# Landing buffers of v apart, three chunks' transposed keys in another PSUM bank, p's sum in PSUM, and a new order of all jobs

## The chip, the core and the metric

The kernel runs on one core of a Trainium2 chip. The core has TensorE (matmuls and their weight loads), VectorE, ScalarE, GpSimd and SyncE, whose queue issues most of the DMAs. The metric is the device time of one execution in microseconds, the median of several runs.

## The reference

Two stages. An attention with a decaying state, and a mixture of four experts over its output:

```python
# r, k, v: (4, 8, 768, 48) f32; w, u: (8, 48)
for t in range(S):
    kt, vt, rt = k[:, :, t], v[:, :, t], r[:, :, t]
    cur = einsum('bhd,bhe->bhde', u[None] * kt, vt)
    y[:, :, t] = einsum('bhd,bhde->bhe', rt, state + cur)
    state = w[None, :, :, None] * state + einsum('bhd,bhe->bhde', kt, vt)
x = y.transpose(0, 2, 1, 3).reshape(3072, 384)
p = domain_probs / (domain_probs.sum(-1, keepdims=True) + 1e-09)     # (3072, 4)
for e in range(4):                                                   # w1: (4, 384, 1024), w2: (4, 1024, 384)
    out += p[:, e:e + 1] * (maximum(x @ w1[e], 0.0) @ w2[e])
```

## The kernel before

The sequence is cut into 24 chunks ci of 128 tokens: batch ci % 4, position ci // 4, so chunks 0 to 3 are the first chunks of the four batches. Each chunk passes these jobs. Its r, k and v are loaded (Rt, Kt, Vt; 192 KB each). `scale` multiplies r and k by powers of w into RK_sb. `T` transposes them (keys are half 1, r half 0) on TensorE, by DMA from chunk 8 on, and `Tout` copies the result from PSUM to RKT in SBUF. `At` is the product of r and keys in the two banks of At_all, `mask` masks it into AtM (two halves, VectorE). `Y` multiplies it by v (Vb, a bf16 copy) and adds the state's part. The u term goes beside this: `ruk_a` (r times k), `ruk_b` (times u), both on GpSimd but for chunk 0, `dcoef` (a sum over 48, VectorE), `dv` (times v, GpSimd), and `Yout` adds dv to y. `Sm`, `Sv`, `S` advance the state.

The experts come in super-chunks of four chunks. For the first two, `X` transposes y on TensorE and `Xout` copies it to xTe. For later ones ScalarE multiplies y by p (`Xs`, line 621) and a DMA transposes each half of the result (`Xout`, line 632). `l1` is x @ w1 (hT_ps), `relu` runs on ScalarE, `l2` is h @ w2 (out_ps), `ev` multiplies it by p. The weights arrive in f32 in pieces of 3, 3 and 2 blocks (w1e0.1 is piece 1 of expert 0's w1) through four staging slots, and `cast` turns each piece into bf16. From the third super-chunk on, sums and differences of blocks replace some of the products. p is transposed (`pt`) and normalized (`pn`, lines 386 to 389) once.

PSUM has eight banks: two in At_all, one for transposes (tr), one for y, states and w (ys), and four general ones (mm). The general ones serve u, the powers of w, p, l1, l2, the transposed y and the filler matmuls alike. A buffer is handed on when the last reader of what was in it is done, which the waiting engine sees as a semaphore.

No engine chooses its next instruction. All 1437 jobs stand in one written list, PLAN; each entry is a job's number in base 62 and the letter of an engine (T TensorE, V VectorE, A ScalarE, P GpSimd, S SyncE's queue). Each engine works off its own entries in the list's order. SPINS puts filler matmuls ahead of named jobs on TensorE: n // 4 of 128x512 and n % 4 of 128x128. They compute nothing that is used. Planner tokens (slots, takes, drops) describe buffers to the program that made the list; the tiles' own buffer counts are in the pool calls. For the two kinds of landing buffers these are:

```python
                t = work.tile([128, H, D], F32, tag=n, bufs=NIN, name=n)
                    tl["in", ci] = work.tile([128, 2, H, D], F32, tag="in", bufs=NIN, name="RKin")
        load_job((n, ci), (0.965, 64), run, (("inp", ci),))
```

Of the kernel before, what the change touches and what calls it, by code (L numbers as in the profile page):

```python
# [18 lines left out]
def kernel(  # L19
# [28 lines left out]
    NIN = 4  # L48
    NRK = 4
# [82 lines left out]
    p_sum = consts.tile([128, TOTC, 1], F32)  # L132
# [70 lines left out]
    slots = dict(inp=NIN, wst=NST, RKT=4, AtM=2, Ysb=3, ruk=3, dv=3, Vb=4, At=2, tr=1, ys=1,  # L203
# [53 lines left out]
    def load_in(n, ci):  # L257
# [3 lines left out]
        def run():  # L261
            if n == "Vt":
                t = work.tile([128, H, D], F32, tag=n, bufs=NIN, name=n)
            else:
                if ("in", ci) not in tl:
                    tl["in", ci] = work.tile([128, 2, H, D], F32, tag="in", bufs=NIN, name="RKin")
                t = tl["in", ci][:, 1 if n == "Kt" else 0]
            tl[n, ci] = t
            nc.sync.dma_start(t, SRC[n][b, :, sl, :].transpose([1, 0, 2]))
        load_job((n, ci), (0.965, 64), run, (("inp", ci),))  # L270
# [108 lines left out]
    def c_pt():  # L379
        tl["pp"] = psum.tile([128, E, TOTC], F32, tag="mm", bufs=4, name="p_ps")  # L380
# [3 lines left out]
    def c_pn():  # L384
        pp = tl["pp"]
        nc.vector.reduce_sum(p_sum, pp.rearrange("p e n -> p n e"), axis=AX.X)
        nc.vector.tensor_scalar(p_sum, p_sum, scalar1=1e-9, scalar2=None, op0=ALU.add)
        nc.vector.reciprocal(p_rec, p_sum)
# [25 lines left out]
    def attention(ci):  # L414
# [43 lines left out]
        def vb(eng):  # L458
# [3 lines left out]
            rk - 0.3 if ci >= SUB else rk, (("Vb", ci),), (("inp", ci),))  # L462
# [10 lines left out]
        job(("dv", ci), {"P": 0.82}, dv, [("dcoef", ci), ("Vt", ci)], rk - 0.4, (("dv", ci),), (("inp", ci),))  # L473
# [9 lines left out]
        else:  # L483
            two = ci < SUB

            def tr(i):
                def run():
                    if two and i:
# [12 lines left out]
            for i in range(2):  # L501
                job(("T", ci, i), {"T": 0.23}, tr(i), [("scale", ci, i)], on_pe,
                    ((("At" if i and two else "tr"), "T", ci),) if i == 0 or two else (),
# [4 lines left out]
            def tout(i):  # L508
                def run(eng):
                    if ("RKT", ci) not in tl:  # L510
                        tl["RKT", ci] = work.tile([128, 2, NP, C], BF16, tag="RKT", bufs=4, name="RKT")
                    if parts == 2:
                        copy_on(eng, tl["RKT", ci][:, i], tl["T", ci, i])
                        if i:
# [4 lines left out]
            if parts == 2:  # L519
# [3 lines left out]
                    rk - 20, (("RKT", ci),), (("At", "T", ci),))  # L523
# [746 lines left out]
    for sc in ORDER_SC:  # L1270
# [11 lines left out]
        for q, m, x in SEQ_OF.get(sc, SEQ_P):  # L1282
# [100 lines left out]
```

## Time and profile before

| | us |
|---|---|
| median of 3 runs | 283.35 |
| lowest and highest run | 282.93, 283.63 |
| span of the profiled execution | 281.5 |
| median less span | 1.85 |
| TensorE busy in the span | 274.8 |
| VectorE, ScalarE, GpSimd busy | 201.3, 182.8, 109.9 |

The span goes from the first to the last instruction of the profiled execution; the device time of a run also holds what lies around it. Busy times are sums over instructions and filler matmuls count as busy.

### The profile page before, as it was taken

To read this page: it belongs to the slowest core of one execution; us is meant where nothing else is said; L and a number is where in the kernel's file an instruction comes from. 1 tells how busy PE (TensorE), PEld (TensorE's weight loads), DVE (VectorE), ACT (ScalarE), POOL (GpSimd) and SP (SyncE) were. 2 spreads that over 40 slices of the span, in tenths; PEclk is the share of its full clock that TensorE was granted. 3 is DMA by queue.
4 is the path that set the end of the run, shared out by engine and by line. 5 is a ranking of instruction groups with operands and counts; after the bars stand their busy time and mean duration, and the time that the engine had idled before them with its cause. 6 is when DMAs were issued, how large, how long until landed. Compare 5 with 4: busy or idle time off the path is not lost.

```text
span 281.5 us, 7035 instructions
## 1 busy us (share of the span) xinstructions
PE 274.8 (98%) x2817; PEld 196.7 (70%) x2817; DVE 201.3 (72%) x368; ACT 182.8 (65%) x350; POOL 109.9 (39%) x137
## 2 busy tenths in 40 slices
PE   7799999999999999999999999999999999999995
PEld 3478567767666454899445899554799644899995
DVE  4968877788798867577354888679996703795672
ACT  5586675888763689644789744688863688653320
POOL 4986334576365479315961425645210000000000
PEclk9999999999999999999999999999999999999999
DMA  7999998998999998678995389967364402000004
GB/s 149 241 307 333 266 325 242 235 245 199 256 197 168 204 207 189 96 145 153 176 179 151 86 157 157 151 138 159 86 88 86 140 2 56 0 2 2 2 15 156
DMA packets 133493, 43.25 MB, mean 154 GB/s; under 512 B 121658, under 2 KB 133436, under 8 KB 133460
## 3 DMA queue, kind: packets, MB, share of 16 engines
q1 hardware_dynamic: 133300, 42.74, 69.5%
q8 instruction: 22, 0.36, 0.6%
q14 instruction: 11, 0.09, 0.1%
q10 hardware_dynamic: 160, 0.05, 0.1%
HBM read 26.79 MB, written 4.72 MB: 112 GB/s over the span
## 4 chain that ended last, share of the span: by engine, by line
PE 93%; DVE 3%; DMA 1%; SPq 1%; ACT 1%; POOL 0%; issue 0%; DVEq 0%; ACTq 0%; POOLq 0%
PE hT_ps L761 35%; PE M_ps L986 26%; PE out_ps L791 7%; PE hT_ps L1216 4%; PE hT_ps L1250 4%; PE out_ps L1233 4%; PE M_two L1164 3%; PE At_all L545 2%; PE Y_ps L592 2%; DMA RKin<-in_r_dram 1%; PE hT_ps L755 1%; PE Y_ps L585 1%; PE St_ps L661 1%; PE At_all L1164 1%; DVE AtM L559 1%; PE At_ps L545 1%
## 5 line engine op out<-in xcount | busy, mean ns | idle before, releaser
L772 ACT ACTIVATE hAll<-hT_ps 128x512 bf16<-128x512 f32 x152 | 85.0, 598 | 19.1 <-PE hT_ps L761 17.1
L761 PE MATMUL hT_ps<-stg,w_sb 128*128 128x512 bf16 x384 | 86.7, 379 | 0.0
L761 PEld LDWEIGHTS <-w_sb 128*128 128x128 bf16 x456 | 42.2, 98 | 45.6
L986 PEld LDWEIGHTS <-hAll 128*128 128x128 bf16 x640 | 52.6, 98 | 1.0
L621 ACT ACTIVATE stg<-dv,p_nat 128x384 bf16<-128x384 f32 x72 | 41.3, 610 | 11.2 <-DMA stg<-stg 8.3
L445 POOL TENSOR_TENSOR ruk<-RKin 128x384 f32<-128x384 f32 x24 | 26.2, 1092 | 22.7 <-DMA RKin<-in_k_dram 16.2
L680 POOL TENSOR_TENSOR S<-Tn,wC 64x192 bf16<-64x192 f32 x32 | 22.4, 700 | 29.9 <-DVE Tn L670 22.0
L1023 ACT COPY o_sb<-M_ps 128x192 f32<-128x192 f32 x35 | 10.9, 316 | 33.7 <-PE M_ps L986 30.2
L986 PE MATMUL M_ps<-w_sb,hAll 128*128 128x192 bf16 x320 | 29.7, 246 | 0.0
L471 POOL TENSOR_TENSOR dv<-Vt,dcoef 128x384 f32<-128x384 f32 x24 | 22.0, 918 | 19.0 <-DVE dcoef L466 10.7
L453 POOL TENSOR_TENSOR ruk<-ruk,U_sd 128x384 f32<-128x384 f32 x23 | 24.1, 1055 | 0.9
L791 PE MATMUL out_ps<-w_sb,hAll 128*128 128x384 bf16 x128 | 22.9, 326 | 0.2 <-DVE p_nat L389 0.2
L934 DVE TENSOR_TENSOR hAll<-hAll 128x1024 bf16<-128x1024 bf16 (+1 forms) x28 | 22.0, 793 | 0.2
L433 DVE TENSOR_TENSOR RK_sb<-RKin,W_both 128x768 bf16<-128x768 f32 x16 | 18.0, 1125 | 1.3 <-DMA RKin<-in_r_dram 1.3
L83 POOL CAST Vb<-Vt 128x384 bf16<-128x384 f32 x16 | 9.1, 567 | 25.1 <-DMA Vt<-in_v_dram 17.2
L761 PE MATMUL hT_ps<-xTe,w_sb 128*128 128x512 bf16 x72 | 18.4, 380 | 0.0
L791 PEld LDWEIGHTS <-hAll 128*128 128x128 bf16 x128 | 12.2, 98 | 8.3 <-issue 0.4
L934 DVE TENSOR_TENSOR hAll<-stg,hAll 128x1024 bf16<-128x1024 bf16 (+1 forms) x14 | 10.5, 765 | 8.3 <-PE M_ps L986 8.0
L986 PE MATMUL M_ps<-w_mix,hAll 128*128 128x192 bf16 x160 | 16.5, 246 | 0.0
L562 DVE TENSOR_TENSOR AtM<-At_all,mask 128x1024 bf16<-128x1024 f32 x8 | 9.7, 1217 | 9.3 <-PE At_all L545 9.3
L986 PE MATMUL M_ps<-o_sb,hAll 128*128 128x192 bf16 x160 | 16.1, 246 | 0.0
L986 PE MATMUL M_ps<-w_sb,stg 128*128 128x192 bf16 x160 | 16.0, 246 | 0.0
(144 smaller groups left out, 440.3 us busy)
## 6 DMA issues: line engine op xcount, KB each, us to landing
stg<-in_moe_w_dram SPq DMA_DIRECT2D x16, 576.0 KB, 6.5
RKin<-in_k_dram SPq DMA_DIRECT2D x24, 192.0 KB, 4.2
Vt<-in_v_dram SPq DMA_DIRECT2D x24, 192.0 KB, 3.9
RKin<-in_r_dram SPq DMA_DIRECT2D x24, 192.0 KB, 3.9
out_dram<-o_sb SPq DMA_DIRECT2D x23, 192.0 KB, 2.3
stg<-in_moe_w_dram SPq DMA_DIRECT2D x8, 384.0 KB, 6.2
stg<-stg SPq DMA_TRANSPOSE x36, 3.1
RKT<-RK_sb SPq DMA_TRANSPOSE x16, 3.2
```

Source lines behind the costliest of these rows:

```text
L433: job(("scale", ci, 0), {"V": SCALE_US}, lambda: nc.vector.tensor_mul(RK[:, :, :, 0:D], tl["in", ci], W_both), [("Rt", ci), ("Kt", ci), (" ...
L445: nc.gpsimd.tensor_mul(tl["ruk", ci], tl["Rt", ci], tl["Kt", ci])
L453: nc.gpsimd.tensor_mul(tl["ruk", ci], tl["ruk", ci], U_sd)
L471: nc.gpsimd.tensor_mul(tl["dv", ci], tl["Vt", ci], tl["dcoef", ci].to_broadcast((128, H, D)))
L621: nc.scalar.mul(o, tl["Ysb", ci], p_nat[:, e, n_p:n_p + 1])
L680: nc.gpsimd.tensor_mul(S_new[pr, :, cl], Tn2[pr, tn_at[ci], :, cl], wC[pr, :, None].to_broadcast((P2, NP, D)))
L761: nc.tensor.matmul(ps[:, 0:n, :].rearrange("p a b -> p (a b)"), w1_sb[:, e, db, fb * 128:(fb + 1) * 128], xTe[:, x0 + db, s0:s0 + n, :].re ...
L772: nc.scalar.activation(hTs[:, fb, s0:s0 + n, :], ps[:, 0:n, :], AF.Relu)
L791: nc.tensor.matmul(ps, relu_tile(e, sc)[:, fb, s, :], w2_sb[:, e, fb, :], start=(fb == 0), stop=(fb == NFB - 1))
L934: nc.vector.tensor_tensor(o, x, y, op=op)
L986: nc.tensor.matmul(tl["P", sc, q, m], st, moving(m, hf, (n + 4) % 8), start=(opens and n == 0 and not (one_bank and m == 7)), stop=(hf == ...
L1164: nc.tensor.matmul(o, st[:, 2 * (3 - n // 2) + n % 2, :], mv, start=(x in ((1, 2) if own else (1,)) and n == 0), stop=(n == 7), skip_group ...
```

## The change

It has four parts. The planner's token inp is split into inp (r and k) and vin (v), with four buffers each. The transposed keys of chunks 1 to 3, which went to a free bank of At_all, go to a general bank. p's sum and the sum plus 1e-9 live in two more columns of p's PSUM tile instead of an SBUF tile. And PLAN and SPINS are new: the last 539 of the 1437 jobs stand in the same order as before, the others do not.

```diff
+    NV = 4
...
-    p_sum = consts.tile([128, TOTC, 1], F32)
...
-                t = work.tile([128, H, D], F32, tag=n, bufs=NIN, name=n)
+                t = work.tile([128, H, D], F32, tag=n, bufs=NV, name=n)
...
-        load_job((n, ci), (0.965, 64), run, (("inp", ci),))
+        load_job((n, ci), (0.965, 64), run, (("vin" if n == "Vt" else "inp", ci),))
...
-        tl["pp"] = psum.tile([128, E, TOTC], F32, tag="mm", bufs=4, name="p_ps")
+        tl["pp"] = psum.tile([128, E + 2, TOTC], F32, tag="mm", bufs=4, name="p_ps")
...
-        pp = tl["pp"]
-        nc.vector.reduce_sum(p_sum, pp.rearrange("p e n -> p n e"), axis=AX.X)
-        nc.vector.tensor_scalar(p_sum, p_sum, scalar1=1e-9, scalar2=None, op0=ALU.add)
-        nc.vector.reciprocal(p_rec, p_sum)
+        pp, p_sum = tl["pp"][:, 0:E], tl["pp"][:, E:E + 2]
+        nc.vector.reduce_sum(p_sum[:, 0].rearrange("p (n o) -> p n o", o=1), pp.rearrange("p e n -> p n e"), axis=AX.X)
+        nc.vector.tensor_scalar(p_sum[:, 1], p_sum[:, 0], scalar1=1e-9, scalar2=None, op0=ALU.add)
+        nc.vector.reciprocal(p_rec.rearrange("p n o -> p (n o)"), p_sum[:, 1])
...
+            own_bank = 0 < ci < SUB
...
-                    if two and i:
+                    if own_bank and i:
+                        tl["T", ci, 1] = psum.tile([128, NP, C], BF16, tag="mm", bufs=4, name="RKT_ps")
+                    elif two and i:
...
-                        if i:
+                        if i and not own_bank:
                             at_free.append(at_of[ci])
...
-    SPINS = {'wmm': 1, 'umm': 1, ('T', 0, 0): 10, ('At', 0): 8, ('T', 2, 0): 16, ('T', 1, 1): 2, ('Y', 0): 3,
-             ('At', 1): 2, ('T', 3, 1): 12, ('T', 2, 1): 4, ('Y', 1): 2, 'wt': 1, ('l1', 0, 0, 3, 0): 1, ('l1',
-             0, 0, 6, 1): 9, ('l1', 0, 0, 0, 0): 8}
+    SPINS = {'wmm': 1, 'umm': 1, ('T', 0, 1): 8, ('T', 0, 0): 8, ('At', 0): 14, ('T', 1, 0): 10, 'wt': 10,
+             ('T', 1, 1): 6, ('At', 1): 3, ('l1', 0, 0, 0, 3): 16}
```

The first three chunks' order changes from 0, 1, 2, 3 to 0, 3, 1, 2. The loads before were K0 V1 R1 R0 K1 R2 R3 V0 K3 K2 w1e0.1 w1e0.2 V2 w1e0.0 p V3 and so on; now they are K3 K0 R3 R0 V0 R1 V3 K1 w1e0.0 K2 p w1e0.1 R2 w1e0.2 V1 w2e0.0. Below are three places of the new order.

ScalarE's queue near the start of the program, before (after the two powers of w; U_sd is the copy of u, RKT the copies of transposed r and k, W_both those of the powers of w):

```order
L368 COPY U_sd_114<-u_ps_155 128x384
L79 COPY RKT_188<-RKT_ps_179 128x512
L366 COPY W_both_113<-W_ps_157 128x384
L366 COPY W_both_113<-W_ps_159 128x384
L79 COPY RKT_218<-RKT_ps_211 128x512
L79 CAST Vb_234<-Vt_161 128x384
L79 COPY RKT_249<-RKT_ps_229 128x512
L370 ACTIVATE hAll_72<-hAll_72 4x128
L79 COPY RKT_292<-RKT_ps_284 128x512
L79 COPY RKT_292<-At_all_120 128x512
L79 CAST w1_sb_70<-stg_73 128x3x384
```

The same place in the new order:

```order
L80 COPY RKT_183<-At_all_119 128x512
L366 COPY W_both_113<-W_ps_156 128x384
L366 COPY W_both_113<-W_ps_162 128x384
L80 COPY RKT_183<-RKT_ps_193 128x512
L80 COPY RKT_222<-RKT_ps_217 128x512
L80 CAST Vb_244<-Vt_139 128x384
L368 COPY U_sd_114<-u_ps_168 128x384
L370 ACTIVATE hAll_72<-hAll_72 4x128
L376 ACTIVATE wC_115<-wt_ps_269 128x4
L80 CAST Vb_272<-Vt_143 128x384
L80 CAST w1_sb_70<-stg_73 128x3x384
L80 COPY RKT_306<-RKT_ps_233 128x512
```

U_sd moved from the first place to the seventh, and chunk 0's keys (RKT_183 from At_all), which VectorE copied, stand ahead of the two copies of w; the first cast of w1 has fewer copies ahead.

VectorE's queue in the same stretch, before (AtM are the masks, y_sb the sums of y and dv, dcoef the u term's sums; p's four operations come some twenty instructions later):

```order
L466 TENSOR_REDUCE dcoef_192<-ruk_164 128x8
L428 TENSOR_TENSOR RK_sb_99<-RKin_146,W_ps_159 128x8x48
L559 TENSOR_TENSOR AtM_216<-At_all_120,mask_94 128x512
L428 TENSOR_TENSOR RK_sb_99<-RKin_150,W_ps_159 128x8x48
L559 TENSOR_TENSOR AtM_216<-At_all_120,mask_94 128x512
L81 COPY RKT_218<-At_all_120 128x512
L466 TENSOR_REDUCE dcoef_269<-ruk_185 128x8
L559 TENSOR_TENSOR AtM_290<-At_all_120,mask_94 128x512 x2
L607 TENSOR_TENSOR y_sb_121<-Y_ps_258,dv_239 128x384
L81 COPY RKT_249<-At_all_120 128x512
L607 TENSOR_TENSOR y_sb_121<-Y_ps_324,dv_304 128x384
```

The same place in the new order:

```order
L466 TENSOR_REDUCE dcoef_214<-ruk_137 128x8
L428 TENSOR_TENSOR RK_sb_99<-RKin_141,W_ps_162 128x8x48
L562 TENSOR_TENSOR AtM_224<-At_all_119,mask_94 128x512 x2
L82 COPY RKT_222<-RKT_ps_239 128x512
L610 TENSOR_TENSOR y_sb_120<-Y_ps_248,dv_257 128x384
L466 TENSOR_REDUCE dcoef_275<-ruk_178 128x8
L562 TENSOR_TENSOR AtM_285<-At_all_119,mask_94 128x512 x2
L82 COPY xTe_312<-xT_ps_308 128x3x128
L82 COPY RKT_306<-RKT_ps_293 128x512
L610 TENSOR_TENSOR y_sb_120<-Y_ps_321,dv_298 128x384
L386 TENSOR_REDUCE p_ps_315<-p_ps_315 128x24
L387 TENSOR_SCALAR p_ps_315<-p_ps_315 128x24
```

Chunk 0's two masks follow each other and its y comes right behind them, ahead of the next chunk's masks; p's operations follow the second chunk's y.

SyncE's queue in the first third of the program, before. L478 are DMA transposes of RK for chunks 11 and 10 and then 13 and 12, L632 those of y times p; the single L632 is the second half of chunk 9, the last one that the third super-chunk's l1 needs:

```order
L632 DMA_TRANSPOSE stg_73<-stg_73 128x6x128 x2
L269 DMA RKin_1591<-in_k_dram 128x8x48
L478 DMA_TRANSPOSE RKT_1603<-RK_sb_99 128x8x128
L269 DMA Vt_1621<-in_v_dram 128x8x48
L269 DMA RKin_1591<-in_r_dram 128x8x48
L632 DMA_TRANSPOSE stg_73<-stg_73 128x6x128
L269 DMA Vt_1646<-in_v_dram 128x8x48
```

The same place in the new order, where the single L635 is the second half of chunk 9 and the two L478 are chunks 10 and 11:

```order
L635 DMA_TRANSPOSE stg_73<-stg_73 128x6x128 x2
L269 DMA Vt_1601<-in_v_dram 128x8x48
L829 DMA out_0_dram<-o_sb_121 128x384
L269 DMA RKin_1624<-in_r_dram 128x8x48
L269 DMA RKin_1624<-in_k_dram 128x8x48
L635 DMA_TRANSPOSE stg_73<-stg_73 128x6x128
L829 DMA out_0_dram<-o_sb_121 128x384
L478 DMA_TRANSPOSE RKT_1674<-RK_sb_99 128x8x128
L478 DMA_TRANSPOSE RKT_1676<-RK_sb_99 128x8x128
```

The RKT transposes of chunks 10 and 11 moved behind chunk 9's second half, and a store of the output stands ahead of it. On TensorE, the first l1 group that reads that half (expert 2 of the third super-chunk) was the twelfth group of the super-chunk and is now the seventh.

## Rows read from the trace of the kernel before

**Rows 1.** Windows of the whole span; columns are named in the first line.

```profile
core 0: us, PE busy (x) PEld busy (x) DVE busy (x) ACT busy (x) POOL busy (x), PEclk, DMA share, GB/s
0.00:16.00 16.00, 12.43 (x104) 6.38 (x106) 10.60 (x29) 8.99 (x16) 11.49 (x23) 1.00 0.92 209
16.00:26.20 10.20, 10.03 (x160) 8.61 (x161) 8.07 (x19) 8.67 (x20) 6.99 (x8) 1.00 1.10 316
26.20:278.60 252.40, 252.35 (x2555) 181.68 (x2554) 182.37 (x321) 165.04 (x316) 91.41 (x108) 1.00 0.68 144
```

**Rows 2.** Windows, filler matmuls alone: us, busy (x), granted clock, DMA share, GB/s.

```profile
0.00:26.20 26.20, 9.59 (x38) 1.00 0.99 251
```

**Rows 3.** Timeline of TensorE: start, duration, instruction, idle before it and its releaser.

```profile
8.58 0.40 PE L545 MATMUL At_all<-RKT 64*128 64x128 bf16 x8 [0.36 <-DVE RKT L81]
...
13.93 0.38 PE L497 MATMUL At_all<-ident,RK_sb 128*128 128x128 bf16 x4 [0.41 <-DVE AtM L559]
...
14.99 0.38 PE L497 MATMUL At_all<-ident,RK_sb 128*128 128x128 bf16 x4 [0.46 <-ACT RKT L79]
...
16.84 0.67 PE L755 MATMUL hT_ps<-xTe,w_sb 128*128 128x128 bf16 x9
...
26.23 1.14 PE L791 MATMUL out_ps<-w_sb,hAll 128*128 128x384 bf16 x6 [0.19 <-DVE p_nat L389]
```

**Rows 4.** Timeline of VectorE, the first 26 us.

```profile
6.55 1.02 DVE L428 TENSOR_TENSOR RK_sb<-RKin,W_ps 128x384 bf16<-128x384 f32 x2 [0.20 <-DMA RKin<-in_r_dram]
...
13.80 0.55 DVE L607 TENSOR_TENSOR y_sb<-Y_ps,dv 128x384 bf16<-128x384 f32 x1
...
24.42 0.26 DVE L386 TENSOR_REDUCE p_sum<-p_ps 128x24 f32<-128x96 f32 x1
24.71 0.83 DVE L387 TENSOR_SCALAR p_sum<-p_sum 128x24 f32<-128x24 f32 x1
25.58 0.30 DVE L388 RECIPROCAL p_rec<-p_sum 128x24 f32<-128x24 f32 x1
25.91 0.26 DVE L389 TENSOR_TENSOR p_nat<-p_ps,p_rec 128x96 f32<-128x96 f32 x1
```

**Rows 5.** Timeline of GpSimd, the first 26 us.

```profile
12.73 1.00 POOL L428 TENSOR_TENSOR RK_sb<-RKin,W_both 128x384 bf16<-128x384 f32 x1 [0.23 <-DMA RKin<-in_k_dram]
...
24.36 1.15 POOL L83 CAST w_sb<-stg 128x1152 bf16<-128x1152 f32 x1 [1.34 <-DMA stg<-in_moe_w_dram]
```

**Rows 6.** Groups of ScalarE, 0 to 45 us: busy, mean ns of one, idle before.

```profile
L79 ACT CAST w_sb<-stg 128x1152 bf16<-128x1152 f32 x3 | 3.5, 1152 | 1.4 <-DMA stg<-in_moe_w_dram 1.3
...
L79 ACT COPY RKT<-RKT_ps 128x512 bf16<-128x512 bf16 x4 | 2.3, 587 | 2.4 <-PE RKT_ps L497 2.3
...
L79 ACT COPY RKT<-RKT_ps 128x1024 bf16<-128x1024 bf16 x2 | 2.0, 1018 | 0.0
...
L366 ACT COPY W_both<-W_ps 128x384 f32<-128x384 f32 x2 | 1.0, 482 | 0.7 <-DVE RK_sb L428 0.7
```

**Rows 7.** Groups of VectorE, 0 to 60 us.

```profile
L559 DVE TENSOR_TENSOR AtM<-At_all,mask 128x512 bf16<-128x512 f32 x15 | 10.1, 684 | 1.7 <-PE At_all L545 1.6
```

**Rows 8.** Timeline of ScalarE, the first 17 us.

```profile
6.15 0.49 ACT L368 COPY U_sd<-u_ps 128x384 f32<-128x384 f32 x1
...
15.06 2.03 ACT L79 CAST w_sb<-stg 128x1152 bf16<-128x1152 f32 x2
```

**Rows 9.** Groups of GpSimd, 5 to 45 us.

```profile
L453 POOL TENSOR_TENSOR ruk<-ruk,U_sd 128x384 f32<-128x384 f32 x5 | 5.1, 1036 | 0.2
```

**Rows 10.** The chain that ended last: start, us, what.

```profile
22.30 0.85 PE hT_ps L755 x15
...
27.36 0.17 PE St_ps L661 x4
27.53 3.41 PE out_ps L791 x21
...
91.47 3.24 PE hT_ps L761 x15
```

**Rows 11.** Timeline of SyncE's queue, near 92 us.

```profile
92.49 1.73 SPq L632 DMA_TRANSPOSE stg<-stg  x1
```

**Rows 12.** DMA issues of the page: count, us from issue to landing.

```profile
stg<-stg SPq DMA_TRANSPOSE x36, 3.1
```

More of the change, by code (lines that the diff above doesn't have):

```diff
@@ L202 @@
              (3, 0), (3, 1))
-    slots = dict(inp=NIN, wst=NST, RKT=4, AtM=2, Ysb=3, ruk=3, dv=3, Vb=4, At=2, tr=1, ys=1,
+    slots = dict(inp=NIN, vin=NV, wst=NST, RKT=4, AtM=2, Ysb=3, ruk=3, dv=3, Vb=4, At=2, tr=1, ys=1,
                  mm=4, xTe=3, oacc=6, Yse0=1, Yse1=1, Tn=2)
@@ L461, in attention @@
         job(("Vb", ci), {"A": 0.42} if ci < SUB else {"P": 0.5} if ci < 8 else VB_ON, vb, [("Vt", ci)],
-            rk - 0.3 if ci >= SUB else rk, (("Vb", ci),), (("inp", ci),))
+            rk - 0.3 if ci >= SUB else rk, (("Vb", ci),), (("vin", ci),))
         def dcoef():
@@ L472, in dv @@
                                  tl["dcoef", ci].to_broadcast((128, H, D)))
-        job(("dv", ci), {"P": 0.82}, dv, [("dcoef", ci), ("Vt", ci)], rk - 0.4, (("dv", ci),), (("inp", ci),))
+        job(("dv", ci), {"P": 0.82}, dv, [("dcoef", ci), ("Vt", ci)], rk - 0.4, (("dv", ci),), (("vin", ci),))
         if dmat:
@@ L502, in attention @@
                 job(("T", ci, i), {"T": 0.23}, tr(i), [("scale", ci, i)], on_pe,
-                    ((("At" if i and two else "tr"), "T", ci),) if i == 0 or two else (),
+                    (((("mm" if own_bank else "At") if i and two else "tr"), "T", ci),) if i == 0 or two else (),
                     behind=(("T", ci, 0),) if i and not two else ())
@@ L522, in attention @@
                 job(("Tout", ci, 1), {"A": 0.53, "V": 0.34}, tout(1), [("T", ci, 1)],
-                    rk - 20, (("RKT", ci),), (("At", "T", ci),))
+                    rk - 20, (("RKT", ci),), (("mm" if own_bank else "At", "T", ci),))
             else:
```

54 lines of the change are left out of this document (27 added, 27 removed).

## The prediction

> **What bounds the kernel now.** I read the windows first: three stretches of the span, cut at 16.0, 26.2 and 278.6 us. TensorE is busy 22.46 us of the first 26.2 [rows 1] and 252.35 of the 252.40 that follow; after its last matmul at 278.6 only copies and a store remain, to 281.5. So TensorE sets the time, at a granted clock of 1.00 throughout, and past 26.2 us there is nothing to win. What can be won lies before. There 9.59 us are filler matmuls [rows 2], and 26.2 - 22.46 = 3.74 us are idle: 13.3 us in which TensorE does nothing that the output needs. A change of order can shorten that start, and it can put new waits into the 252 us without one. The rest of this text weighs these two.
>
> The median of the runs, 283.35 us, is 1.85 above the span of 281.5; I forecast spans and add 1.85.
>
> Next I read the timeline of TensorE in the start, to see what ends its idle time. Three things show [rows 3]. The key transposes of chunks 3 and 2 stand still (0.41, 0.46 us) because their target, a bank of At_all, still holds something that VectorE or ScalarE has to read. The first expert's first l1 matmul runs at 16.84. And the first l2 matmul after the p normalization, at 26.23, was let go by p_nat.
>
> **Part 1, the token for v.** The planner's token inp is split into inp and vin. The two kinds of tile had separate buffers, four each, before (lines 263 and 266). At run time the split does nothing: 0. Its only way to matter is through the new order.
>
> **Part 2, chunks 1 to 3's transposed keys in a general bank.** This removes the two waits of 0.41 and 0.46 us [rows 3] as such. But the four general banks also serve the fillers, W_ps, u_ps, p_ps, xT_ps and hT_ps, and TensorE had filler work or later-released work around them. I count the gain only within the walk below.
>
> **Part 3, p's sum in PSUM.** The four operations took 0.26, 0.83, 0.30 and 0.26 us [rows 4]. The 0.83 (the addition of 1e-9, SBUF to SBUF) ran 24.71 to 25.54, and GpSimd's weight cast ran 24.36 to 25.51 [rows 5]; the two end together. The operations that read p_ps take 0.26. I take 0.26 for the addition and 0.26 to 0.30 for the reciprocal: the chain falls from 1.75 us (24.42 to 26.17) to about 1.15, worth 0.6 on VectorE. Its worth on TensorE is at most what the wait at 26.23 cost there, and with p computed ten us earlier in the new order, nothing waits for it at all. It is in the walk too. Bounds: 0 (if nobody waits) to 0.6.
>
> [...]
>
> **Part 4, the new order in the start.** I walked the first 26 us of the new order instruction by instruction with durations from the rows, and give the steps that decide.
> - Chunk 0's first product comes later. Its second-half RKT copy goes from VectorE to ScalarE, and there stand RKT, W, W, RKT in a row: 0.59 + 0.48 + 0.48 + 0.59 [rows 6]. ScalarE begins at 6.85, so the product starts at 9.05 instead of 8.58 [rows 3]: 0.5 lost.
> - Chunk 0's output comes earlier. Before, y0's addition ran at 13.80 [rows 4], behind the mask products of a second chunk. Now both masks of chunk 0 (0.68 each [rows 7]) follow each other and end at 10.83; with y0 behind them its addition runs at 11.55: 2.2 us earlier.
> - U_sd's copy moves back on ScalarE, from 6.15 [rows 8] to 10.95. GpSimd's ruk product of chunk 3 needs it (1.04 us [rows 9]), VectorE's dcoef comes after that, and only then the masks of chunk 3. Those end at 14.4, although their product is done at 12.7. This is a new wait, and scale of chunk 1 on GpSimd (1.0) is queued behind the same ruk: chunk 1's key transposes start at 13.56, with chunk 0's x behind them.
> - The weights come earlier. Loads land 1.03 us apart ((12.73 - 6.55)/6 from the fourth to the tenth [rows 4, 5]). Before, ten loads of r, k, v stood ahead of the first w1 piece, whose cast starts at 15.06 [rows 8]; now eight do, so it lands at about 13.0. The second w1 piece (0.59 MB at 316 GB/s [rows 1] is 1.9, and one k of 1.03 ahead of it) lands at 15.9 (15.0 to 16.2).
> - So l1 begins at 15.96 instead of 16.84. But ScalarE then holds the second cast (1.15 [rows 6], 15.8 to 16.95) and Xout of chunk 3 behind it (17.45), and the next l1 waits for that until 18.35, with fillers in between.
> - p runs at 15.7 to 16.8 and l2 begins at 23.1, interleaved with the last l1.
>
> The balance at the end of that stretch: when the fourth chunk's x is transposed, at 25.53 in the walk, TensorE has done 72 of the 96 l1 matmuls of the first expert, 9 l2 matmuls and 3 state products. Before, it had 96, 3 and 2 at 26.23, l2's first three counted as done since they preceded p's wait. At 0.85/15 = 0.057, 3.41/21 = 0.162 and 0.17 us each [rows 10], that is -1.36 + 0.97 + 0.17 = -0.22. The new order is thus where the old one was at 25.53 + 0.22 = 25.75 instead of 26.23: **0.5 us gained**. Bounds: each landing shifts it about one for one, -0.6 (second w1 piece at 16.2 and a late U) to +1.4.
>
> **Part 5, the new order after 26 us.** Nothing can be won here, so I looked for margins that become negative, with TensorE taken as never waiting.
> - Chunk 5's RKT copy (1.02) now stands on ScalarE behind a weight cast of 1.15 [rows 6]. In the walk the cast ends at 36.05 and the copy at 37.07, and TensorE wants it at 36.9: 0.2, from 0 to 0.5.
> - The second super-chunk's l1 on the second half of x: TensorE starts that super-chunk at 91.47, and a group of three matmuls takes 3.24/5 = 0.65 [rows 10]. Before, the second half was first used after eleven groups; now after six, at 91.47 + 3.9 = 95.4. Its last transposing DMA was issued at 92.49 before [rows 11], 3.1 from issue to landing [rows 12]: 95.6, which would be a little late. In the new order the two RKT transposes that stood ahead of it stand behind, and I place its issue at 90.7 and its landing at 93.8: margin 1.6. Cost 0, from 0 to 1.9 (landing 3.1 after the old row's end at 94.22, that is 97.3).
> - The products of the same super-chunk run within 0.15 of their inputs: 0.1, from 0 to 0.4.
> - The last 539 of the 1437 jobs stand in the same order; the end costs 0.
>
> **Sum.** 281.5 - 0.5 + 0.3 = 281.3 span, 283.15 in the runs' terms; I write 283.1. Its own range is 282.4 to 283.8.
>
> **Rivals.**
> - *The start gains more* (p. 0.29): the second w1 piece lands at 15.0, so its cast and Xout of chunk 3 end 0.8 earlier, and the fillers in front of the next l1 shrink with it. -0.5 - 0.8 + 0.2 = -1.1: 282.2. For it: the old order fills 9.6 us with fillers, so much is slack. Against: chunk 3's late masks hold y3 anyway.
> - *The transposed y of the second half comes late* (p. 0.17): issued no earlier than before, it lands at 97.0 (between 95.6 and 97.3) where TensorE wants it at 95.4. -0.5 + 0.2 + 1.6 = +1.3: 284.6. The gain is gone from a landing at 95.7, and the change is measurably slower from 96.6. For it: the y comes from the same chunk 9, and a store of the output now stands ahead of it in the queue. Against: the two RKT transposes that stand behind it now.
> - *Slower in the start* (p. 0.11): U's late copy puts chunk 3's masks, and through them X of chunk 3, past the second cast; the walk is 1.2 too early from 14 us on. -0.5 + 1.2 + 0.3 = +1.0: 284.3. For it: GpSimd's queue has no gap there.
> - *The change does not do what it says* is true of part 1 already, and lies within the forecast: part 1 gives 0, and part 3 alone at most 0.6 of VectorE's time.
>
> **How the numbers follow.** The forecast's case holds 0.43, the others 0.29, 0.17 and 0.11. A difference of 0.3% (0.85 us) is about what a measurement of this kernel can tell from none. Of the forecast's 0.43 I put 0.05 below 282.5 and 0.02 above 284.2, of the first rival's 0.29 I put 0.24 below, of the two slower ones' 0.28 I put 0.24 above. So faster 0.29, same 0.45, slower 0.26. The range: from 281.8 (the start's bound of -1.4 with 0.15 of stalls behind it, less a few tenths of the runs' own spread) to 284.7 (the late transpose at its price), leaving 0.1 at each side.
>
> **What would show it.** Right: first l1 near 16.0, p's four operations near 0.26 each and before 17 us, no wait on At_all in the transposes of chunks 1 to 3; chunk 3's masks more than 1.5 us behind their product; TensorE without idle time from 26 us on but for some tenths near 37 and 95. Wrong: an idle gap over 0.5 us at the second super-chunk's l1, or in the second expert's; a fall of the granted clock in the first 16 us, where fillers are set anew; or first l1 as late as before.

## The result and the profile after

| | us |
|---|---|
| before, median of 4 runs (lowest, highest) | 283.46 (282.93, 283.63) |
| changed, median of 4 runs (lowest, highest) | 286.21 (285.90, 286.93) |
| ratio, 95% interval | 1.0108 [1.0094, 1.0121] |
| span of the profiled execution, before and changed | 281.5, 284.0 |

The changed kernel is 1.1% slower, above the range that was given. The windows of the changed kernel, cut where [rows 1] were cut and further at 60, 100 and 160 us (columns: stretch, us, busy time of TensorE, of its weight loads, VectorE, ScalarE and GpSimd with instructions, granted clock, DMA share, GB/s):

```profile
0.00:16.00 16.00, 12.49 (x106) 6.78 (x107) 10.07 (x28) 8.45 (x16) 9.92 (x21) 1.00 1.01 206
16.00:26.20 10.20, 9.50 (x149) 7.76 (x144) 8.72 (x21) 7.53 (x16) 7.77 (x8) 1.00 1.09 281
26.20:60.00 33.80, 33.53 (x357) 22.68 (x358) 23.55 (x40) 25.07 (x42) 17.97 (x21) 1.00 1.07 274
60.00:100.00 40.00, 38.26 (x327) 23.61 (x329) 27.23 (x42) 25.49 (x46) 19.23 (x23) 1.00 1.05 208
100.00:160.00 60.00, 59.35 (x553) 39.66 (x560) 44.38 (x62) 43.91 (x87) 33.99 (x37) 1.00 0.87 154
```

Before, TensorE was idle for 0.05 us after 26.2 us. Now it is idle for 0.27 + 1.74 + 0.65 = 2.66 us from 26.2 to 160 alone, and most of it stands between 60 and 100 us. Not all of that is waiting: old_order_refilled below, whose view has no wait there, still shows 0.21 + 0.26 + 0.27 = 0.74 us in the same windows, so about 1.9 us is the new order's. The granted clock is 1.00 in every row, so the clock is not the cause. The view of waits names those gaps (TensorE, 26 to 281 us; us in total, times, longest):

```profile
PE At_ps L548 <- DMA RKT<-RK_sb: 1.0, 1, 1.0
PE hT_ps L764 <- DMA stg<-stg: 0.4, 1, 0.4
PE At_all L548 <- DMA RKT<-RK_sb: 0.2, 1, 0.2
```

All three are transposing DMAs that land too late: the keys of chunk 9 (its product, At_ps, follows chunk 8's, which doesn't wait), the second half of chunk 9's y, and a later pair of chunks' keys. (The view has two more rows of 0.2 us; at these a matmul's record seems to be missing from a group, so they say little.) TensorE's timeline has them, and its start, to compare with [rows 3]:

```profile
8.89 0.40 PE L500 MATMUL RKT_ps<-ident,RK_sb 128*128 128x128 bf16 x4 [1.60 <-DVE RK_sb L428]
9.97 0.40 PE L548 MATMUL At_all<-RKT 64*128 64x128 bf16 x8
...
16.61 0.67 PE L758 MATMUL hT_ps<-xTe,w_sb 128*128 128x128 bf16 x9
...
73.96 0.40 PE L548 MATMUL At_ps<-RKT 64*128 64x128 bf16 x8 [1.01 <-DMA RKT<-RK_sb]
...
96.77 3.40 PE L764 MATMUL hT_ps<-stg,w_sb 128*128 128x512 bf16 x15 [0.41 <-DMA stg<-stg]
...
148.21 0.40 PE L548 MATMUL At_all<-RKT 64*128 64x128 bf16 x8 [0.18 <-DMA RKT<-RK_sb]
```

VectorE's timeline has p's four operations, which answer to [rows 4], and a wait of 1.40 us that was not foreseen:

```profile
8.27 0.56 DVE L428 TENSOR_TENSOR RK_sb<-RKin,W_ps 128x384 bf16<-128x384 f32 x1 [1.40 <-ACT W_both L366]
...
16.30 0.25 DVE L386 TENSOR_REDUCE p_ps<-p_ps 128x24 f32<-128x96 f32 x1
16.59 0.19 DVE L387 TENSOR_SCALAR p_ps<-p_ps 128x24 f32<-128x24 f32 x1
16.81 0.31 DVE L388 RECIPROCAL p_rec<-p_ps 128x24 f32<-128x24 f32 x1
17.15 0.26 DVE L389 TENSOR_TENSOR p_nat<-p_ps,p_rec 128x96 f32<-128x96 f32 x1
...
64.90 1.97 DVE L433 TENSOR_TENSOR RK_sb<-RKin,W_both 128x768 bf16<-128x768 f32 x2
```

One more line of the page matters, on which the prediction did not rest: the DMA queue that carries nearly everything (before, 42.74 of 43.24 MB; columns: packets, MB, the packets' time as a share of 16 engines' span). Before and changed:

```profile
q1 hardware_dynamic: 133300, 42.74, 69.5%
```

```profile
q1 hardware_dynamic: 133300, 42.74, 73.2%
```

The same packets with the same bytes take a share that is 5% larger in the changed kernel, of a longer span. The change puts the transfers in another order, but alters none of them.

### The profile page after: what moved, and what is told of

It is laid out like the page before. It is cut to its first block, busy times and chain, and to the rows that moved or that the text cites. A ratio compares the mean times of both kernels' runs of the same rounds, so it can differ in the third digit from the quotient of the medians.

```text
span 284.0 us, 7000 instructions
## 1 busy us (share of the span) xinstructions
PE 273.6 (96%) x2794; PEld 196.2 (69%) x2814; DVE 200.6 (71%) x368; ACT 183.1 (64%) x352; POOL 111.4 (39%) x135
## 2 busy tenths in 40 slices
DMA packets 133492, 43.24 MB, mean 152 GB/s; under 512 B 121658, under 2 KB 133436, under 8 KB 133460
## 3 DMA queue, kind: packets, MB, share of 16 engines
q1 hardware_dynamic: 133300, 42.74, 73.2%
## 4 chain that ended last, share of the span: by engine, by line
PE 80%; DMA 9%; SPq 3%; POOL 2%; issue 2%; ACT 1%; DVE 1%; POOLq 0%; ACTq 0%; DVEq 0%
PE hT_ps L764 31%; PE M_ps L989 23%; PE out_ps L794 6%; DMA stg<-in_moe_w_dram 4%; PE hT_ps L1253 4%; DMA RKT<-RK_sb 3%; PE hT_ps L1219 3%; PE out_ps L1236 3%; SPq L269 3%; PE M_two L1167 3%; DMA stg<-stg 1%; PE Y_ps L595 1%; PE St_ps L664 1%; PE Y_ps L588 1%; PE At_all L548 1%
## 5 line engine op out<-in xcount | busy, mean ns | idle before, releaser
L471 POOL TENSOR_TENSOR dv<-Vt,dcoef 128x384 f32<-128x384 f32 x24 | 22.7, 948 | 35.2 <-DVE dcoef L466 28.3
L445 POOL TENSOR_TENSOR ruk<-RKin 128x384 f32<-128x384 f32 x24 | 26.8, 1121 | 17.3 <-DMA RKin<-in_r_dram 17.1
L683 POOL TENSOR_TENSOR S<-Tn,wC 64x192 bf16<-64x192 f32 x32 | 20.8, 648 | 29.2 <-DVE Tn L673 28.0
L453 POOL TENSOR_TENSOR ruk<-ruk,U_sd 128x384 f32<-128x384 f32 x23 | 25.8, 1126 | 2.3 <-ACT U_sd L368 1.1
L794 PE MATMUL out_ps<-w_sb,hAll 128*128 128x384 bf16 x128 | 23.7, 326 | 0.0
L937 DVE TENSOR_TENSOR hAll<-hAll 128x1024 bf16<-128x1024 bf16 (+1 forms) x28 | 23.1, 835 | 0.2
L764 PE MATMUL hT_ps<-xTe,w_sb 128*128 128x512 bf16 x66 | 16.9, 379 | 0.5 <-DVE RK_sb L428 0.2
L433 DVE TENSOR_TENSOR RK_sb<-RKin,W_both 128x768 bf16<-128x768 f32 x16 | 17.2, 1079 | 0.1
L740 DVE SCALAR_TENSOR_TENSOR o_sb<-out_ps,p_nat,o_sb 128x384 f32<-128x384 f32 x18 | 10.9, 612 | 8.1 <-PE out_ps L1236 5.4
L610 DVE TENSOR_TENSOR dv<-Y_ps,dv 128x384 f32<-128x384 f32 x18 | 9.9, 553 | 9.0 <-PE Y_ps L595 4.5
```

The source lines that it names most:

```text
L433: job(("scale", ci, 0), {"V": SCALE_US}, lambda: nc.vector.tensor_mul(RK[:, :, :, 0:D], tl["in", ci], W_both), [("Rt", ci), ("Kt", ci), (" ...
L445: nc.gpsimd.tensor_mul(tl["ruk", ci], tl["Rt", ci], tl["Kt", ci])
L453: nc.gpsimd.tensor_mul(tl["ruk", ci], tl["ruk", ci], U_sd)
L471: nc.gpsimd.tensor_mul(tl["dv", ci], tl["Vt", ci], tl["dcoef", ci].to_broadcast((128, H, D)))
L683: nc.gpsimd.tensor_mul(S_new[pr, :, cl], Tn2[pr, tn_at[ci], :, cl], wC[pr, :, None].to_broadcast((P2, NP, D)))
L764: nc.tensor.matmul(ps[:, 0:n, :].rearrange("p a b -> p (a b)"), w1_sb[:, e, db, fb * 128:(fb + 1) * 128], xTe[:, x0 + db, s0:s0 + n, :].re ...
```

## The experiments

Two questions were open: which part costs the time, and why loads became slower. The first four kernels take the change apart; the next four remove single waits of the new order; then come the addresses; the last six combine. Ratios are to the kernel before on the same chip, with 95% intervals.

**old_order** is the changed kernel with the lists of before.

```diff
-    SPINS, PLAN = (those of the changed kernel)
+    SPINS, PLAN = (those of before)
```

> The changed kernel's tiles (token, general bank for the keys of chunks 1 to 3, p in PSUM) under the old order and old fillers. Theory (the loss comes from the new order behind 31 us): 0 to 0.4 us under the kernel before, because p's wait at 26.2 us shrinks; 283.2. Rival (the general bank costs waits): 0.5 us or more above before, with new idle time of TensorE before l1 groups in the first 30 us.

283.82 us, 1.0014 [0.9999, 1.0030]; its profiled span is 281.0, and from 24 us on its view of waits has no row for TensorE. So parts 1 to 3 add no wait behind the start that this view shows, and most of the loss is the order's. But the highest of its runs, 285.16, is far above the highest of before (284.24), and the DMA queue's share is 73.7%, as in the changed kernel.

**old_p_only** is the kernel before with part 3 alone (p's sum in PSUM, the SBUF tile p_sum gone).

```diff
-    p_sum = consts.tile([128, TOTC, 1], F32)
...
-        tl["pp"] = psum.tile([128, E, TOTC], F32, tag="mm", bufs=4, name="p_ps")
+        tl["pp"] = psum.tile([128, E + 2, TOTC], F32, tag="mm", bufs=4, name="p_ps")
```

> The kernel before with p's sum and the sum plus 1e-9 in PSUM, nothing else. Both theories: the addition takes 0.2 to 0.3 us instead of 0.83, and the l2 matmul that waited for p starts 0.36 us earlier; so -0.3 us, 283.15, if all of this reaches the end; 0 if some other wait takes its place.

284.16 us, 1.0031 [1.0019, 1.0043]: slower, by an edit to four small operations that took 1.65 us together in [rows 4] and 1.01 in the changed kernel. The DMA queue's share is 75.1%. This made the removed tile the suspect.

**old_start_new_rest** and **new_start_old_rest** are the changed kernel with mixed lists: the first 191 jobs in the old order and the others in the new one; and the last 1229 in the old order, behind 208 that follow the new one with a few exchanges.

```diff
-    PLAN = (new)
+    PLAN = (old, first 191) + (new, others)
```

> The first 191 jobs (to about 31 us) in the old order with the old fillers, all others in the new order. Theory (loss behind 31 us): the same stalls near 72.7, 96, 131 and 147 us, 2.2 us in all, less up to 0.4 from p: 285.3. Rival (the new start costs it, in timed executions more than in the profiled one): 283.2.

295.22 us, 1.0427 [1.0403, 1.0451]. One wait of 6.0 us for a weight cast stands at the seam, so the time tells nothing of either half. The view of waits does: for chunk 9's keys (1.0 us) and for the second half of its y (0.9 us) TensorE waits behind the old start too, so these waits belong to the new order's rest.

```diff
-    PLAN = (new)
+    PLAN = (new, others) + (old, last 1229)
```

> The first 190 jobs in the new order with the new fillers, all others in the old order. Theory (loss behind 31 us): no stall behind 31 us, and a start that is 0.2 us shorter than before: 283.2. Rival (the new start costs it): 285 or more.

284.58 us, 1.0046 [1.0033, 1.0059]. Here too a weight cast is late at the seam (1.4 us at an l2). With 1.4 us of the seam's own in it, it is still 0.0062 (1.8 us) below the changed kernel: the new order's rest is worse than the old one's, and the new start by itself seems to cost little.

**product89_later** moves the job At of chunk 9 (the products of chunks 8 and 9) on TensorE behind the next l2 group, and the y of chunk 8 behind one more, so that the late keys have that group's time to land.

```diff
 (l1,3,1,4,0)
+(l2,2,3)
 (At,9)
-(l2,2,3)
 (l1,2,1,4,1)
 (l2,2,1)
+(l2,2,4)
 (Y,8)
-(l2,2,4)
```

> The changed kernel, with the product of chunks 8 and 9 (and its three masks) one group of eight l2 matmuls later on TensorE, and the y of chunk 8 one such group later too. Theory (TensorE loses 1.0 to 1.15 us at 72.7 because the DMA-transposed keys of chunk 9 land there 1 us after it asks): that wait falls to 0 and the time falls by 1.0, to 285.2. Rival (a stall moved is a stall kept: y of chunk 8 or the masks take its place): 286.2, with a new wait at Y or At between 73 and 80 us.

286.81 us, 1.0124 [1.0107, 1.0142]. The wait of 1.0 us is gone, and the time is no lower, for the next ones grew:

```profile
PE hT_ps L764 <- DMA stg<-stg: 0.9, 1, 0.9
PE At_all L548 <- DMA RKT<-RK_sb: 0.3, 1, 0.3
```

**second_half_later** lets three l1 groups that don't need chunk 9's second half go ahead of the first one that does.

```diff
 (l1,0,2,1,0)
+(l1,0,2,7,0)
+(l1,1,2,5,0)
+(l1,0,2,2,0)
 (l1,2,2,5,0)
...
-(l1,0,2,7,0)
 (At,11)
 (l1,3,2,4,0)
-(l1,1,2,5,0)
-(l1,0,2,2,0)
 (Y,10)
```

> The changed kernel, with three l1 groups of the third super-chunk that read the first half of x put ahead of the first group that reads the second half (which is then the tenth instead of the seventh group). Theory (the wait of 0.41 us at 96 us, 0.58 in all, is for the transposed y of chunk 9): it goes, 285.7. Rival (the DMA transposes behind it are late by the same amount and the wait moves to the product of chunks 10 and 11): 286.2.

286.58 us, 1.0120 [1.0107, 1.0133]. The wait for that half is gone; two others of 0.4 and 0.2 us, for relu's copy and for a mask, appear where the three groups were taken away.

**both_later** has both edits.

```diff
 (the two diffs above)
```

> Both of the last two edits. Theory: the two gains add up, 1.6 us, 284.6; what is left over the kernel before is then the two small waits at 131 and 147 us and what the end adds. Rival: less than 0.5 us.

287.08 us, 1.0137 [1.0113, 1.0160]. No wait over 0.3 us is left behind 26 us, and it isn't faster. Its profiled execution, 288.43 us, the longest of its six, also lost time in the start (below, at changed_refilled).

**keys89_earlier** goes to the cause of the first wait: chunk 8's r is issued ahead of a weight piece, its scale runs ahead of a weight cast, and its transposes go ahead of y's.

```diff
 (Kt,8)
+(Rt,8)
 (wst,2,2,0)
-(Rt,8)
...
-(cast,1,2,2)
 (scale,9,0)
 (scale,8,0)
+(cast,1,2,2)
...
-(Xout,6,0)
 (T,8,1)
 (T,9,1)
+(Xout,6,0)
```

> The changed kernel with the keys of chunks 8 and 9 made earlier, and TensorE's order as it is: r of chunk 8 is loaded ahead of the first piece of expert 2's w2, both scale operations stand ahead of the weight cast on VectorE, both RKT transposes ahead of the transposed y of chunk 6 in SyncE's queue. Theory (the load's place among the weight pieces makes the keys late): the transposes are issued 1.2 to 1.5 us earlier and the wait of 1.0 us at 72.7 goes, 285.2. Rival (the DMA engines' backlog decides, whatever the order of issue): wait unchanged, 286.2.

286.81 us, 1.0129 [1.0113, 1.0144]. The keys' wait is gone from the list, and three others take its place:

```profile
PE hT_ps L764 <- DMA stg<-stg: 1.1, 2, 0.8
PE hT_ps L764 <- DVE w_sb L82: 0.4, 1, 0.4
PE At_all L548 <- DMA RKT<-RK_sb: 0.3, 1, 0.3
```

These four point one way: from 60 to 100 us the new order seems to have no reserve on the queue of loads and on VectorE, so that what is pulled forward pushes something else back. The views show the waits that moved; that the reserve is the reason is argued from them.

**The addresses.** p_sum took 96 bytes of each partition. It is allocated ahead of p_rec, the weights, the staging slots, the output and the landing buffers, so without it all of those start 96 bytes lower. In the program as built the first landing buffer of r and k starts at byte 176192 before and at 176096 now: 64 and 224 bytes past a multiple of 256. Four kernels add a tile that nothing uses, to move all of these together and nothing else; which of the moved buffers matters was not taken apart.

**before_shifted** is the kernel before with 32 unused bytes (landing buffers 96 past a multiple of 256), **before_256** with 192 (at a multiple).

```diff
     p_rec = consts.tile([128, TOTC, 1], F32)
+    unused = consts.tile([128, 8, 1], F32)
```

> The kernel before with an unused SBUF tile of 32 bytes a partition behind p_rec, nothing else. Theory (addresses): the DMA queue's share rises from 69.5% to about 74%, the first loads land 1.05 us apart, and the time rises by 0.5 to 1.2 us, 284.1. Rival: 283.2, no change.

```diff
+    unused = consts.tile([128, 48, 1], F32)
```

> The kernel before with an unused SBUF tile of 192 bytes a partition, which puts staging slots and landing buffers at multiples of 256 bytes (before: 64 past one). [...] Rival (only multiples of 64 matter): the same time and share as before.

283.98 us, 1.0022 [1.0012, 1.0033], and 283.49 us, 1.0008 [0.9999, 1.0017]. The queue's line of each, before_shifted first:

```profile
q1 hardware_dynamic: 133300, 42.74, 73.5%
```

```profile
q1 hardware_dynamic: 133300, 42.74, 65.9%
```

Nothing but the addresses differs, and the same packets take 73.5%, 69.5% or 65.9%. How far one set of addresses varies is seen in the pages of all kernels: 71.2 to 75.1% in the ten whose buffers start 224 or 96 bytes past a multiple of 256, 68.3 to 70.0% in the eight at 64 past, 65.9 and 67.9% in the two at a multiple (the second is old_order_256). So 96 and 224 stand clearly apart from 64, and a multiple of 256 by little. There the kernel before gains nothing, which fits loads that are hidden; at the shifted addresses it loses 0.2%. Windows of 8 to 16 us show the loads of the start, before and then before_shifted:

```profile
8.00:16.00 8.00, 6.04 (x80) 3.72 (x80) 6.35 (x14) 5.07 (x10) 7.69 (x9) 1.00 1.04 261
```

```profile
8.00:16.00 8.00, 6.22 (x82) 3.80 (x79) 6.36 (x13) 5.00 (x10) 7.64 (x9) 1.00 1.27 247
```

The DMA share there is 1.27 instead of 1.04, and yet 247 GB/s are moved instead of 261.

**changed_refilled** and **old_order_refilled** are the changed kernel and old_order with 96 unused bytes in p_sum's place, which puts every buffer back where it was before.

```diff
+    unused = consts.tile([128, TOTC, 1], F32)
     p_rec = consts.tile([128, TOTC, 1], F32)
```

> The changed kernel with an unused SBUF tile of 96 bytes a partition where p_sum stood. The change took that tile out, so that every tile behind it (weights, staging slots, landing buffers) begins 96 bytes lower and at 32 bytes past a multiple of 64 instead of at one. Theory (the shifted addresses slow every load, 1.05 us apart instead of 0.95, and the new order's waits at 72.7, 96, 131 and 147 us are the late data): the DMA queue's share goes back from 73.2% to about 69.5%, most of the 2.2 us of waits goes, 283.5. Rival (the order makes the waits): 286.2.

> The changed kernel's tiles under the old order, with the same unused tile of 96 bytes. Theory (addresses): loads as fast as before and the wait for p gone, 282.9, and less spread than without the tile (282.8 to 285.2). Rival (order alone matters): 283.8 as without it.

285.53 us, 1.0067 [1.0051, 1.0084], and 282.78 us, 0.9982 [0.9970, 0.9993]. The queue's share is 68.3% and 68.7%. So the addresses cost 0.41% under the new order and 0.32% under the old one (the ratios' differences to the changed kernel and to old_order, each to some 0.2%; about 1.2 and 0.9 us), and in before_shifted 0.22%. With them back in place the first three parts make the kernel faster by 0.5 us. Under the new order one wait over 0.3 us is left, and it did not shrink, so chunk 9's keys are not late because of the addresses:

```profile
PE At_ps L549 <- DMA RKT<-RK_sb: 1.1, 1, 1.1
```

Its start was a surprise. The profiled run of changed_refilled took 287.22 us (span 285.4), where its other runs took 284.10 to 285.65. TensorE's timeline of the first ten us, of the changed kernel and then of changed_refilled:

```profile
4.00 1.22 PE L348 MATMUL w_ps<-hAll 128*128 128x384 f32 x2
...
6.46 0.40 PE L500 MATMUL At_all<-ident,RK_sb 128*128 128x128 bf16 x4
```

```profile
4.33 1.65 PE L349 MATMUL w_ps<-hAll 128*128 128x384 f32 x2 [0.42 <-ACT hAll L345]
...
8.12 0.63 PE L501 MATMUL At_all<-ident,RK_sb 128*128 128x128 bf16 x4
```

w's load landed 0.3 us later there (ScalarE begins on it at 3.75 instead of 3.43 us). TensorE stood idle for 0.42 us, and its matmuls up to 8.5 us then took longer (0.63 for the four transposes instead of 0.40; the two of u, not shown, 1.59 instead of 0.86). The transposes are 1.66 us later. both_later shows the same. The granted clock of 5 to 8.5 us reads 1.00 in both kernels, so that column does not show why, and the cause stays open.

**refilled_scale_early** takes the wait of 1.40 us out of the start: chunk 0's scale of r on VectorE is written ahead of the copy of the same PSUM bank (W_ps) on ScalarE, the second of two.

```diff
-1DA1MV
+1MV1DA
```

> The changed kernel with the 96 bytes refilled, and VectorE's scale of chunk 0's r ahead of ScalarE's copy of the same bank W_ps in the written order, so that VectorE no longer waits for the copy (1.40 us in the changed kernel) and chunk 0's product starts about 0.9 us earlier. Theory (this wait is a part of the start's cost): 0.5 to 0.9 us under the refilled kernel's 285.5: 284.8. Rival (the start's end is set by the second w1 piece and GpSimd's chain, as I walked it): 285.5.

The first transposes on which it had been waiting run at 7.16 instead of 8.89. The time is 285.21 us, 1.0078 [1.0053, 1.0104], which can't be told from 1.0067. From 26.2 to 160 us TensorE is idle for 2.59 us, against 2.66 in the changed kernel, and its view has 1.2 us for chunk 9's keys and 0.4 for the second half of its y. So the good addresses do not shorten these waits; at 26.2 us TensorE is ahead of the changed kernel by 0.8 us (75.8 l1 and 15.0 l2 products against 72 and 11.4, at the prediction's prices), but this has the early scale in it too.

**refilled_scale_product** adds product89_later's edit, **refilled_all_later** that of second_half_later too.

```diff
 (refilled_scale_early, and product89_later)
```

> The last kernel, with the product of chunks 8 and 9 one group later too. Theory (with the loads at their old pace the wait of 1.1 us at the product is one by itself, and no later one takes its place): another 1.0 us, 283.8. Rival (the chain of chunk 9's y behind it passes the lateness on, as with the slow loads): 284.8.

```diff
 (refilled_scale_early, product89_later, and three l1 groups ahead of the second half's)
```

> The last kernel, with the first four l1 groups of the third super-chunk's second half three groups later and three groups of the first half ahead of them, group counts around the products kept. Theory: the wait near 96 us is gone already with the loads at their old pace, so nothing: 283.8. Rival (it had only passed out of sight): 283.4.

284.78 us, 1.0058 [1.0044, 1.0072], and 285.04 us, 1.0063 [1.0045, 1.0081]. Neither can be told from changed_refilled. Both are clearly slower than old_order_refilled.

**old_order_256** is old_order with 288 unused bytes, so that its landing buffers start at a multiple of 256.

```diff
+    unused = consts.tile([128, 72, 1], F32)
```

> The old order with p's sum in PSUM, the general bank for three chunks' keys, and an unused tile of 288 bytes that puts staging slots and landing buffers at multiples of 256 bytes. Theory (loads are hidden in the old order, so their pace beyond that of before buys nothing): as with 96 bytes, 282.8. Rival: 282.3.

282.33 us, 0.9973 [0.9959, 0.9987]: with parts 1 to 3, the old order and a multiple of 256 this has the lowest time of the study, 0.7 us below before. It can't be told from old_order_refilled.

**new_85_old_rest** and **old_85_new_rest** join the two orders near 85 us instead (the buffers refilled; the first of them with the early scale).

```diff
-    PLAN = (new)
+    PLAN = (new, others) + (old, last 931)
```

> The first 480 jobs (to about 85 us) in the new order with VectorE's early scale, all others in the old order, the 96 bytes refilled. Theory (each stretch of the new order asks for late data at places of its own): the wait of 1.1 us at the product of chunks 8 and 9 stays, those at 96 and 131 us are gone since the old order asks for the second half of x four groups later; with a start 0.5 shorter, 283.6. Rival (all waits behind 85 us come from what was put off before): they appear in the old rest too, 284.8.

```diff
-    PLAN = (new)
+    PLAN = (old, first 488) + (old, some reordered, to the join) + (new, last 883)
```

> The first 488 jobs in the old order with the old fillers, all others in the new order, the 96 bytes refilled. Theory: no wait up to 85 us and 0.5 us won by p, then waits of 0.5 to 1.0 us at the second half of x near 94 us and 0.3 near 131 us: 283.6. Rival (what is late there was put off before 85 us): no waits, 282.7.

286.72 us, 1.0125 [1.0112, 1.0138], and 286.92 us, 1.0120 [1.0085, 1.0156]. Both are slower than either order by itself, so seams make waits of their own and the split of the time stays open. One part came as expected: the wait for chunk 9's keys is in new_85_old_rest (1.27 us, at 74 us) and not in old_85_new_rest, so it belongs to the new order ahead of 85 us. One row of old_85_new_rest shows the price of a long gap; TensorE's timeline, and the windows around it:

```profile
97.42 5.10 PE L765 MATMUL hT_ps<-stg,w_sb 128*128 128x512 bf16 x15 [2.27 <-DMA stg<-stg]
```

```profile
95.00:100.00 5.00, 2.73 (x10) 1.01 (x10) 0.00 (x0) 1.68 (x3) 2.84 (x5) 0.83 1.08 226
100.00:110.00 10.00, 9.95 (x66) 4.66 (x66) 5.08 (x7) 7.84 (x15) 2.46 (x3) 0.92 0.55 116
```

The granted clock falls below 1.00 with this gap of 2.27 idle us: it reads 0.83 from 95 to 100 us and 0.92 from 100 to 110, and 1.00 from 80 to 95 and from 110 to 130. The fifteen matmuls took 5.10 us, where they take 3.40 in the changed kernel's timeline (the row at 96.77).

## Why the prediction was wrong

**The sum that the runs give.** In shares of the time before: the first three parts with the buffers in place, -0.18% (old_order_refilled); the new order on top, +0.85% (1.0067 less 0.9982, about 2.4 us); the addresses under the new order, +0.41% (1.2 us). Together that is +1.08%, the measured ratio, as it has to be, since each term is a difference between two of these kernels. The forecast had -0.5 us for parts 1 to 4 and +0.3 for part 5. So the largest error is the price of the new order (parts 4 and 5), and the second a term, the addresses, that the forecast did not have at all.

**The bound.** That nothing can be won after 26.2 us and much can be lost was right. The loss is where the text looked for it, past 26 us, but larger.

**Parts 1 and 2.** Nothing waits for a bank of At_all in the key transposes of chunks 1 to 3 any more, as forecast, and old_order has no new waits behind the start. They were never run without part 3.

**Part 3, the step that left out a term.** The durations came as said: 0.25, 0.19, 0.31 and 0.26 us, the addition's 0.19 while a product of GpSimd's ran beside it (16.03 to 17.03 us). Its worth lies within "0 to 0.6": parts 1 to 3 together bring some 0.5 us in old_order_refilled, and its own share of that was not measured apart. But the step costed the four operations and nothing else. It removed an SBUF tile, and that moved every buffer allocated behind it; that term, 0.9 to 1.2 us, was put at nothing without a reason, and it outweighs the gain: old_p_only, which has part 3 alone, is slower than before.

Why an address costs transfer time is in no view. The shares are all that was measured: 69.5% before at 64 bytes past a multiple of 256, 73.2% in the changed kernel at 224 and 73.5% in before_shifted at 96, 65.9 and 67.9% in the two kernels at a multiple, near the 68.3 to 70.0% of those at 64. To count from multiples of 256 was the author's choice, and no run has its buffers at any other distance than these four.

The reciprocal took 0.31 us from PSUM against 0.30 from SBUF in [rows 4]. The addition's 0.83 had GpSimd's cast beside it and its 0.19 a product of GpSimd's; no run takes apart whether the cast or the tile's place made the difference.

**Part 4, the start.** The walk gave 0.5 us of gain; the trace has 0.2. By the prediction's own prices, at 26.2 us TensorE has done 72 l1, about 11.4 l2 and 3 state products, against 96, 3 and 2 before: -24 x 0.057 + 8.4 x 0.162 + 0.17 = +0.2. The walk's first step failed: its four copies in a row on ScalarE from 6.85 on leave no room for a wait. But VectorE's scale of chunk 0's r reads a PSUM bank that the second of ScalarE's two copies of W_ps reads too, and it waited for that copy (1.40 us). Chunk 0's product ran at 9.97 instead of the walk's 9.05, the first l1 at 16.61 instead of 15.96. refilled_scale_early removes the wait, but shows no gain in the runs. The walk had no place for a late w either: where it lands 0.3 us later (the profiled run of changed_refilled), the first key transposes run 1.66 us later. The other late steps of the walk are right in kind: U_sd came late (11.63) and GpSimd's product behind it (12.26). One sign did not come: chunk 3's masks were to stand more than 1.5 us behind their product, but they began at 13.76, some 0.2 us behind the end of a product that was itself late (13.13 instead of the walk's end near 12.7). Neither rival on the start came: the profiled start is 0.2 us shorter, not 1.3 shorter and not 0.7 longer.

**Part 5, the step that was mis-sized.** It summed to 0.3 us; the windows have 2.66 up to 160 us, about 1.9 of it waits. (What this part calls the second super-chunk, beginning at 91.47, is the third one, chunks 8 to 11.)
- The keys of chunk 9 cost 1.0. The text names no margin for them; if they are among "the products of the same super-chunk" (0.1, from 0 to 0.4), that term is the one that was too small. SyncE's queue shows the way (start, duration, transfer, number):

```profile
57.71 1.37 SPq L269 DMA_DIRECT2D RKin<-in_r_dram  x1
59.17 2.33 SPq L289 DMA_DIRECT2D stg<-in_moe_w_dram  x2
...
67.62 2.63 SPq L478 DMA_TRANSPOSE RKT<-RK_sb  x2
...
92.99 1.75 SPq L635 DMA_TRANSPOSE stg<-stg  x1
```

Chunk 8's r is issued at 57.71 behind a weight piece; both chunks' scales run at 64.90 on VectorE, behind a weight cast; their transposes are issued one behind the other from 67.62, chunk 9's at about 69.0. TensorE asks for chunk 9's at 72.95. Before, they were issued at 59.31 and 64.74, and TensorE asked from 71.28 on:

```profile
59.31 1.32 SPq L478 DMA_TRANSPOSE RKT<-RK_sb  x1
...
64.74 1.24 SPq L478 DMA_TRANSPOSE RKT<-RK_sb  x1
```

```profile
71.28 0.40 PE L545 MATMUL At_all<-RKT 64*128 64x128 bf16 x8
```

So the second of the two was issued 4.2 us later, for a product only 1.4 us later (72.95 against 71.51, the row behind this one). The chain of waits has the landings (start, us):

```profile
68.96 4.95 DMA RKT<-RK_sb
...
92.99 3.64 DMA stg<-stg
```

- The second half of chunk 9's y was a rival, with 0.17, and its mechanism came: issued no earlier than before, at 92.99 instead of the forecast's 90.7, it landed at 96.63 (the rival said 97.0). But it cost 0.4 and not 1.6: by then TensorE was itself late, and asked at 96.4 instead of 95.4.
- Chunk 5's copy, 0.2: no wait shows there.
- The wait of 0.2 at 148 us was not listed at all.

A transposing DMA was priced at 3.1 us from [rows 12], the median of one kind. Under the new order those that TensorE waits for took 3.6 to 5.0, and with the old addresses back it was 5.0 for chunk 9's keys, so it is not the addresses.

**What stays open.** refilled_scale_product has the early scale, the later product and the old addresses, and still stands 0.0076 above old_order_refilled. In the profiled executions its last matmuls begin at 278.86 instead of 277.06, 1.8 us later; 1.1 us of that is idle time of TensorE between 26.2 and 160 us (1.87 against 0.74 in the windows), and the rest is in no view. It is not the start: by the prices above both have done the same work at 26.2 us (76.7 l1, 15.0 l2 and 3 state products against 96, 9.0 and 2). Each edit of the order behind 26 us moved waits and brought no time, so which of the 898 jobs that stand elsewhere causes how much is not settled.

## What to carry to other kernels

Before a tile is removed or resized, look at what is allocated behind it: an edit that has nothing to do with transfers can move all landing buffers to worse addresses, and the profile's line for the DMA queue (here the same 133300 packets and 42.74 MB, at 69.5% before and 75.1% in old_p_only) shows it. Where an engine is busy throughout, a new order is judged by the smallest margin of every transfer that this engine waits for, with the latency of the loaded queue (3.6 to 5.0 us here) and not the median (3.1); and a single late transfer that is pulled forward can push back the next one, as in the four kernels above.

## What the hardware showed that was not expected

- With the buffers behind one small tile at 96 or 224 bytes past a multiple of 256, the same 133300 packets took 71.2 to 75.1% of the 16 DMA engines' time, against 68.3 to 70.0% at 64 past and 65.9 and 67.9% at a multiple.
- A load that landed 0.3 us late, and with it 0.42 idle us of TensorE at 4 us, went with matmuls that took up to 1.8 times as long until 8.5 us (1.59 us for the two of u instead of 0.86), with a granted clock printed as 1.00.
- An instruction of VectorE that only reads a PSUM bank waited 1.40 us until ScalarE's copy out of that bank was done, when it stood behind it in the list; in refilled_scale_early, where it stands ahead of that copy, the transposes of its result ran at 7.16 us instead of 8.89.
